# A state-space scan and an ELU layer on one core: seven Strassen products in float32, or three passes over 12-bit words

## The chip, the cores and the metric

The kernel runs on one core of a Trainium2 chip. The metric is the time on the device in microseconds (us). A core has TensorE (PE, with PEld for its weight loads), VectorE (DVE), ScalarE (ACT), GpSimd (POOL) and SyncE (SP), which issues most DMAs. Each engine takes its instructions strictly in the order in which the kernel wrote them, and waits on semaphores for what another engine has to finish first.

## What is computed

Two things in a row, cut to what matters:

```python
# 1. scan: x (4, 8, 768, 32), a (4, 8, 768), B and C (4, 8, 768, 16)
M = (C @ B.T) * L                      # L[i, j] = exp(cum_i - cum_j), j <= i
y = M @ x + (C @ state) * exp(cum)     # state is carried from chunk to chunk
# 2. two layers over the 3072 tokens, 256 features each (8 heads x 32)
h = y @ w_in                           # w_in (256, 2048)
g = np.where(h > 0, h, np.exp(np.minimum(h, 0)) - 1)
out = g @ w_out                        # w_out (2048, 256)
```

The weights are given in 64 bits; the kernel turns them into float32 first.

## The kernel before

The 3072 tokens are 12 blocks of 256 tokens (`BLK`), numbered 0 to 11. For each block the scan makes y as `yT` (features on the partitions), the first layer makes `g_of`, the second layer the output rows. All is one program in an order written out by hand (`manual_schedule`): the scan of later blocks, the first layer of this pair and the second layer of the pair before are woven into each other, piece by piece.

- **Start.** Blocks 0 to 3 use plain float32 products in the first layer (`l1`, L658). Meanwhile the 64-bit weights are loaded in 16 pieces and converted (`w_take`, `w_give`; the magnitude `mag`, the sign `sgn`, the low part, joined by POOL at L239).
- **Blocks 2 and 3** weave `l1` with the second layer of 0 and 1 (`l2`, L779). With block 3, `more_sums` makes sums of the weights for what follows: DVE those of w_out (L706), POOL those of w_in.
- **Pairs (4,5), (6,7), (8,9), (10,11).** This is the loop `for n in range(4, NP, 2)`. Its 16 half steps k do the first layer of the pair by Strassen's scheme: `front`, `mid` and `back` do seven products of 128 x 128 by 128 x 256 for each of eight feature pairs i (all through `part_product`, L730), with sums joined on DVE (L747, L755, L763) and one copy on ACT (L740). `sum_y` makes the sums of y on POOL. `begin_elu` and `elu` make g: Relu (L671) and Exp (L678) on ACT, the join on DVE (L680). `sum_t1` subtracts quarters of g on POOL (L807).
- **Second layer in the same loop**, for the pair before (`second`, L853): seven products in two halves of four chunks each, also by Strassen's scheme. One `next` of this generator, called by `l2s`, does one chunk: two products of 128 x 128 by 128 x 128. Between them POOL subtracts (L795) and adds (L831), DVE adds what stands in PSUM (L831), and ACT copies two of the results (L860, L872).
- **Scan of the next pair in the same loop**: decays by ACT (`decay`, L512, 32 pieces of 64 columns twice, masked by POOL at L517), at k = 10 `scores` (L532), `sums` of the states (L562), `weigh` (DVE, L541) and `states`, and at k = 13 `across` (L607) and `inside` (L626), whose results ACT copies to `yT` (L643).

PSUM has eight banks of 128 x 512 float32. Seven of them are one ring that all temporary results share in the order in which they are asked for; the eighth belongs to the second layer:

```python
p_a = ctx.enter_context(tc.tile_pool(name="ps_a", bufs=7, space=PSUM))
p_o = ctx.enter_context(tc.tile_pool(name="ps_o", bufs=1, space=PSUM))
def psum(shape, name):
    return p_a.tile(shape, F32, tag="a", name=name)
```

A tile asked for waits until the one that had its bank seven requests earlier has been read for the last time. `scores` asks for four banks, `sums` for two, `across` for four, a Strassen step for two.

Of the kernel before, what the change touches and what calls it, by code (L numbers as in the profile page):

```python
# [12 lines left out]
BF16 = mybir.dt.bfloat16  # L13
ALU = mybir.AluOpType
ACT = mybir.ActivationFunctionType

P = 128
Q = 64
BLK = 2 * P
CW = 256  # L20

# [7 lines left out]
def kernel(  # L29
# [56 lines left out]
    la0 = const.tile([P, 2, P], F32, name="la0")  # L86
# [50 lines left out]
    def load_x(n, piece=None):  # L137
        b, g = place(n)
        st[n]["x"] = raw.tile([P, 2, NH * D], F32, tag="xr", name="xr", bufs=4)
        for u in range(2):  # L140
            sl = slice((2 * g + u) * P, (2 * g + u + 1) * P)
            nc.sync.dma_start(  # L142
                out=st[n]["x"][:, u].rearrange("p (h d) -> p h d", d=D),
                in_=x[b, :, sl, :].rearrange("h s d -> s h d"))
            if piece is not None and u == 0:
                w_load(piece)


    w_in = const.tile([P, KC, DF], F32, name="w_in")
# [3 lines left out]
    for i in range(DF // CW):  # L153
        pieces.append((
            w_in[:, :, i * CW:(i + 1) * CW],
# [6 lines left out]
    W_AHEAD = 8  # L162
# [18 lines left out]
    def w_abs(i, cols=slice(None)):  # L181
        if i in (1, 2) or cols.start:
            w_abs_of[i, cols.start] = psum([P, 2, CW], "ps_mag").bitcast(U32)
        if i not in w_mag:
            w_mag[i] = (ffn.tile([P, 2, CW], U32, tag="tmp", name="mag", bufs=1) if i == 2 else
                        conv.tile([P, 2, CW], U32, tag="mag", name="mag"))
# [19 lines left out]
    def w_sign(i, cols=slice(None), eng=nc.vector):  # L206
        if i not in w_sgn:
            w_sgn[i] = conv.tile([P, 2, CW], U32, tag="sgn", name="sgn")
# [54 lines left out]
    keep = const.tile([P, 2, P], F32, name="keep")  # L263
# [30 lines left out]
    heads = [const.tile([P, NH, N], F32, name=f"heads{n}") for n in range(2)]  # L294
# [31 lines left out]
    F0 = const.tile([P, 2, P], F32, name="F0")  # L326
# [68 lines left out]
    def scaled(n, eng):  # L395

        s = st[n]
        s["sc"] = sc = att.tile([P, 2, NH, N], F32, tag="sc", name="sc", bufs=2)
# [15 lines left out]
    def turn(n):  # L414
# [8 lines left out]
        s["bt"] = att.tile([P, 2, 2, P], F32, tag="bct", name="bct", bufs=2)[:, 0]  # L423
# [7 lines left out]
    def turn_exp(n, eng=nc.vector):  # L431

        s = st[n]
        s["cts"] = att.tile([P, 2, P], F32, tag="cts", name="cts", bufs=2)
# [180 lines left out]
    def inside(y, *ns):  # L615


        for t in range(2):
# [16 lines left out]
            for v in range(2):  # L635
                k = shift(n, v)
                for at in (0, k) if k else (0,):
                    count, src = P - k, (at + k) % P
                    to, src = out[at:at + count, :, :, Q * v:Q * v + Q], y[t][v][src:src + count]
                    if t and n == 1:  # L640
                        nc.vector.tensor_copy(to, src)
                    else:
                        nc.scalar.copy(out=to, in_=src)  # L643
# [6 lines left out]
    def l1(n, i, parts=1):  # L650

        ps = psum([P, 2, BLK], "ps_h")
        for j in range(2):
            m = 2 * i + j
            for part in range(parts):
                toks = slice(part * BLK // parts, (part + 1) * BLK // parts)
                for k in range(KC):
                    nc.tensor.matmul(  # L658
                        out=ps[:, j, toks], lhsT=w_in[:, k, m * P:(m + 1) * P],
# [52 lines left out]
    w_parts = w_in.rearrange("p k (i r c) -> p k r i c", r=2, c=P)  # L712
    a_in = a11, a12, a21, a22 = [w_parts[:, k, r] for r in range(2) for k in range(2)]
    w_parts = w_out.rearrange("p (i k) (r c) -> p k r i c", k=2, c=P)
    a_out = [w_parts[:, k, r] for r in range(2) for k in range(2)]
    s_in, s_out = [], []

    y_sums = {}

    def sum_y(n):  # L720
        t = y_sums[n] = conv.tile([P, 4, BLK], F32, tag="w64", name="y_sum", bufs=W_AHEAD)
        b11, b12, b21, b22 = (
            yT[n // 2][:, k, at].rearrange("p u i -> p (u i)") for k in range(2) for at in range(2))
        for r, (in0, in1) in enumerate(((b12, b11), (b22, t[:, 0]), (b22, b12), (b21, t[:, 1]))):
            nc.gpsimd.tensor_tensor(out=t[:, r], in0=in0, in1=in1, op=ALU.subtract)

    open_ = {}

    def part_product(out, lhsT, rhs, first=False):
        nc.tensor.matmul(  # L730
            out=out, lhsT=lhsT, rhs=rhs, start=first, stop=True, skip_group_check=True)
# [3 lines left out]
    def front(n, i):  # L735
        c1, c2 = psum([P, 2, BLK], "ps_h"), psum([P, 2, BLK], "ps_h")
        t = y_sums[n]
        part_product(c1[:, 0], a11[:, i], yT[n // 2][:, 0, 0].rearrange("p u i -> p (u i)"), True)
        u = conv.tile([P, 3, BLK], F32, tag="mag", name="u_sum")
        nc.scalar.copy(out=u[:, 0], in_=c1[:, 0])  # L740
        part_product(c2[:, 0], s_in[0][:, i], t[:, 1], True)
        part_product(c2[:, 1], a21[:, i], t[:, 0])
        open_[n, i] = c1, c2, u

    def front_sums(n, i):
        c1, c2, u = open_[n, i]
        nc.vector.tensor_tensor(  # L747
            out=u[:, 1:3], in0=c2, in1=u[:, 0].unsqueeze(1).to_broadcast([P, 2, BLK]), op=ALU.add)

    def mid(n, i):  # L750
        c1, c2, u = open_[n, i]
        b21 = yT[n // 2][:, 1, 0].rearrange("p u i -> p (u i)")
        part_product(c1[:, 0], a12[:, i], b21)
        part_product(c2[:, 0], s_in[1][:, i], y_sums[n][:, 2])
        nc.vector.tensor_tensor(out=c1[:, 1], in0=c2[:, 0], in1=u[:, 2], op=ALU.add)  # L755
        lag.append((n, i, c1))

    def back(n, i):
        c1, c2, u = open_.pop((n, i))
        b22 = yT[n // 2][:, 1, 1].rearrange("p u i -> p (u i)")  # L760
        part_product(c2[:, 0], a22[:, i], y_sums[n][:, 3])
        part_product(c2[:, 1], s_in[2][:, i], b22)
        nc.vector.tensor_tensor(out=c2, in0=c2, in1=u[:, 0:2], op=ALU.add)  # L763
        lag.append((n + 1, i, c2))
# [7 lines left out]
    def l2(n, j, half=None):  # L772
# [10 lines left out]
        if j == MC // 2 - 1 and half != 0:  # L783
            ob = ffn.tile([P, 2, DM], F32, tag="ob", name="ob", bufs=1)
# [12 lines left out]
    def quarters(n, i):  # L797


        A, B = g_of[n, i], g_of[n + 1, i]  # L800
        if n < 4:
            return A[:, 0], A[:, 1], B[:, 0], B[:, 1]
        return A[:, 0], B[:, 0], B[:, 1], A[:, 1]
# [273 lines left out]
    ends = {(3, 13): (4, 5), (4, 13): (6, 7), (6, 13): (8, 9), (8, 13): (10, 11)}  # L1077

    def end_of_two(n, step):
# [227 lines left out]
```

## Time and profile before

| | |
|---|---|
| median of three runs | 354.9 us (354.79 to 355.4) |
| span of the profiled execution | 353.3 us |
| what lies around the span, against the median | 1.6 us |
| granted TensorE clock | 1.000 |
| first product of the loop over pairs | 115.1 us from the span's start |
| last products, L839, the end of the second layer | 349.8 us from the span's start |

A profile's group row names the line, the engine, the operation, what is written from what, the shape and the count; then the busy time of the group and the mean ns of one instruction; then the idle time of that engine just before them, with what ended it. A timeline row has the start, the length and the instructions merged into it. A matmul's row shows its end with the pipeline's drain, so the rate is read from start to start. A float32 product appears as two matmul records.

### The profile page before, as it was taken

The numbers are of one execution on the slowest core, as the hardware profiler recorded it, in microseconds if no ns is written. First come the engines' busy times: TensorE is split into PE (matmuls) and PEld (weight loads), VectorE is DVE, ScalarE is ACT, GpSimd is POOL, SyncE is SP. The second block draws the span as 40 slices with busy tenths as digits, with TensorE's granted clock in tenths as the row PEclk, the third lists the DMA queues.
The fourth block names the chain that finished last, engine by engine and source line by source line (L and its number), as shares of the span: only waits on it lengthen the run. The fifth ranks groups of instructions, "written<-read, shape, count | busy, mean of one in ns | idle before, by whom it ended". The sixth has DMA issues, their size and how long they took to land.

```text
span 353.3 us, 9964 instructions
## 1 busy us (share of the span) xinstructions
PE 346.3 (98%) x3958; PEld 312.6 (88%) x3958; DVE 239.4 (68%) x497; ACT 204.3 (58%) x497; POOL 231.5 (66%) x366
## 2 busy tenths in 40 slices
PE   8799999999999999999999999999999999999996
PEld 5579888888888999999999999999999999999996
DVE  4898979863999768684677684677684565656212
ACT  4789989787435577535677535586635444535100
POOL 5554554563676997887377788468687545465883
PEclk9999999999999999999999999999999999999999
DMA  8988987550450500145500145600000100000001
GB/s 147 235 213 216 284 206 183 118 98 30 71 142 2 121 1 2 19 99 125 123 0 2 13 82 137 134 3 0 2 2 4 60 3 0 2 0 30 32 2 59
DMA packets 72726, 26.49 MB, mean 75 GB/s; under 512 B 57768, under 2 KB 67560, under 8 KB 72680
## 3 DMA queue, kind: packets, MB, share of 16 engines
q1 hardware_dynamic: 70360, 25.60, 31.5%
q8 instruction: 31, 0.51, 0.6%
q10 hardware_dynamic: 2320, 0.26, 0.5%
q14 instruction: 15, 0.12, 0.1%
HBM read 22.51 MB, written 3.34 MB: 73 GB/s over the span
## 4 chain that ended last, share of the span: by engine, by line
PE 92%; DVE 2%; DMA 2%; SPq 2%; issue 0%; POOL 0%; ACT 0%; DVEq 0%; POOLq 0%; ACTq 0%
PE ps_o L853 35%; PE ps_h L730 28%; PE ps_h L658 15%; PE ps_o L779 8%; PE ps_y L626 2%; DMA w<-in_moe_w_in_dram 2%; PE ps_g L532 2%; PE ps_y L607 1%; PE ps_st L562 1%; SPq L169 1%; PE ps_o L839 1%; POOL w_in L239 0%; DVE sgn L214 0%; DVE ps_mag L222 0%; SPq L142 0%
## 5 line engine op out<-in xcount | busy, mean ns | idle before, releaser
L671 ACT ACTIVATE e<-ps_h 128x512 f32<-128x512 f32 x96 | 57.1, 595 | 91.0 <-DVE ps_h L755 49.3
L853 PEld LDWEIGHTS ps_o<-w_out,g 128*128 128x128 f32 x640 | 79.9, 192 | 2.9
L853 PE MATMUL ps_o<-w_out,g 128*128 128x128 f32 x640 | 81.0, 275 | 0.0
L680 DVE SCALAR_TENSOR_TENSOR g<-e,ps_h 128x512 f32<-128x512 f32 x96 | 65.1, 680 | 14.3 <-ACT e L678 13.7
L658 PE MATMUL ps_h<-yT,w_in 128*128 128x256 f32 (+1 forms) x272 | 60.4, 370 | 2.9 <-POOL w_in L239 2.9
L678 ACT ACTIVATE e<-e 128x512 f32<-128x512 f32 x96 | 60.9, 635 | 2.0
L807 POOL TENSOR_TENSOR g<-g 128x256 f32<-128x256 f32 x33 | 24.0, 728 | 54.8 <-DVE g L680 54.7
L658 PEld LDWEIGHTS ps_h<-yT,w_in 128*128 128x128 f32 x272 | 48.4, 190 | 10.4 <-POOL w_in L239 4.0
L512 ACT ACTIVATE L<-L,ncum 128x64 f32<-128x64 f32 x160 | 41.1, 338 | 0.2
L853 PE MATMUL ps_o<-w_sum,g 128*128 128x128 f32 x304 | 39.9, 275 | 0.0
L853 PEld LDWEIGHTS ps_o<-w_sum,g 128*128 128x128 f32 x304 | 38.5, 192 | 1.1
L763 DVE TENSOR_TENSOR ps_h<-ps_h,u_sum 128x512 f32<-128x512 f32 x32 | 22.4, 698 | 24.0 <-PE ps_h L730 23.8
L730 PE MATMUL ps_h<-yT,w_in 128*128 128x256 f32 x128 | 38.5, 383 | 0.0
L730 PE MATMUL ps_h<-y_sum,w_in 128*128 128x256 f32 x128 | 38.2, 380 | 0.0
L730 PE MATMUL ps_h<-y_sum,w_sum 128*128 128x256 f32 x128 | 38.1, 379 | 0.0
L517 POOL TENSOR_SCALAR_AFFINE_SELECT L<-L 64x512 f32<-64x512 f32 x40 | 28.0, 700 | 11.9 <-ACT L L512 10.6
L747 DVE TENSOR_TENSOR u_sum<-ps_h,u_sum 128x512 f32<-128x512 f32 x32 | 22.1, 689 | 14.7 <-ACT u_sum L740 11.0
L755 DVE TENSOR_TENSOR ps_h<-ps_h,u_sum 128x256 f32<-128x256 f32 x32 | 13.8, 433 | 25.9 <-PE ps_h L730 25.8
L779 PE MATMUL ps_o<-w_out,g 128*128 128x256 f32 x128 | 30.7, 382 | 0.0
L795 POOL TENSOR_TENSOR t<-g 128x256 f32<-128x256 f32 x40 | 28.9, 754 | 0.2
L795 POOL TENSOR_TENSOR g<-g,t 128x256 f32<-128x256 f32 x40 | 28.8, 753 | 0.3
L795 POOL TENSOR_TENSOR g<-t,g 128x256 f32<-128x256 f32 x40 | 27.9, 733 | 1.1 <-PE ps_o L853 1.1
(120 smaller groups left out, 534.8 us busy)
## 6 DMA issues: line engine op xcount, KB each, us to landing
L<-flat SPq DMA_DIRECT2D x20, 256.0 KB
w<-in_moe_w_out_dram SPq DMA_DIRECT2D x8, 512.0 KB
w<-in_moe_w_in_dram SPq DMA_DIRECT2D x7, 512.0 KB
xr<-in_x_dram SPq DMA_DIRECT2D x24, 128.0 KB
out_dram<-c_sum SPq DMA_DIRECT2D x9, 256.0 KB
bc<-in_B_dram SPq DMA_DIRECT2D x24, 64.0 KB
bc<-in_C_dram SPq DMA_DIRECT2D x22, 64.0 KB
ec<-flat_exp SPq DMA_DIRECT2D x10, 128.0 KB
```

Source lines behind the costliest of these rows:

```text
L512: nc.scalar.activation(L[:, h, u], L[:, h, u], ACT.Exp, bias=ncum[:, u, row:row + 1])
L517: nc.gpsimd.affine_select(out=part, in_=part, pattern=[[0, 4], [0, 2], [1, Q]], compare_op=ALU.is_ge, fill=0.0, base=0, channel_multiplier=-1)
L658: nc.tensor.matmul(out=ps[:, j, toks], lhsT=w_in[:, k, m * P:(m + 1) * P], rhs=yT[n // 2][:, k, n % 2].rearrange("p u i -> p (u i)")[:, toks],
L671: nc.scalar.activation(begun[0], lag[0][2], ACT.Relu, scale=-1.0)
L678: nc.scalar.activation(e, e, ACT.Exp, scale=-1.0)
L680: nc.vector.scalar_tensor_tensor(out=g_of[n, i], in0=e, scalar=1.0, in1=ps, op0=ALU.subtract, op1=ALU.max)
L730: nc.tensor.matmul(out=out, lhsT=lhsT, rhs=rhs, start=first, stop=True, skip_group_check=True)
L763: nc.vector.tensor_tensor(out=c2, in0=c2, in1=u[:, 0:2], op=ALU.add)
L779: nc.tensor.matmul(out=o_of[n][:, ts], lhsT=g_of[n, j][:, m % 2, ts * P:(ts + 1) * P], rhs=w_out[:, m], start=(m == 0 and ts == 0), stop=( ...
L795: nc.gpsimd.tensor_tensor(out=out, in0=in0, in1=in1, op=ALU.subtract)
L807: eng.tensor_tensor(out=b12, in0=b12, in1=b11, op=ALU.subtract)
L853: nc.tensor.matmul(out=ps[:, ts], lhsT=b[:, ts * P:(ts + 1) * P], rhs=a[:, i], start=(i == chunk[0] and ts == 0), stop=(i == chunk[-1]), s ...
```

## The change

The first layer of blocks 4 to 11 is done with three products of words in place of Strassen's seven products. A weight w is written as w1 + w0 with w1 rounded to 12 bits (`words_of_w`), y likewise as high and low words (`words_of_y`); y has been multiplied by 2^12 when it was copied out of PSUM. `l1_words` multiplies high by high, low by low, and (high + low) by (high + low), the last into a bank of its own, as Karatsuba's scheme does. All operands have the type float32r and the products have 512 columns, both blocks of the pair at once. The two banks are joined by ACT and DVE, and the ELU follows; the last step of it (`end_words`) is written one tile later.

Other parts that move with it: `w_in` is no longer one tile but eight pieces in a ring of nine that later holds `w0`; the ring `w64` has 11 buffers instead of 8 and later holds the weights' words; `mag` and `sgn` of the conversion take their buffers from the rings of g; `y1` and `y0` have one buffer, `both` shares the two buffers of `yT`; `first` and `bct` gather small tiles; x has three buffers in place of four; `load_bc` for later blocks is called two steps later; `end_of_two`, which ends the scan of a pair and now splits its y, stands at k = 14.

The diff, cut to its core:

```diff
-        st[n]["x"] = raw.tile([P, 2, NH * D], F32, tag="xr", name="xr", bufs=4)
+        st[n]["x"] = raw.tile([P, 2, NH * D], F32, tag="xr", name="xr", bufs=3)
...
-    W_AHEAD = 8
+    W_AHEAD = 11
...
+                    elif n < 4:
+                        nc.scalar.copy(out=to, in_=src)
                     else:
-                        nc.scalar.copy(out=to, in_=src)
+                        nc.scalar.activation(to, src, ACT.Copy, scale=WORD)
...
-    def sum_y(n):
...
-    def front(n, i):
...
-    def front_sums(n, i):
...
-    def mid(n, i):
...
-    def back(n, i):
...
+    def words_of_w(i):
+        w = pieces[i][0]
+        both = conv.tile(
+            [P, 2, KC, CW], F32R, tag="w64", name="w_words", bufs=W_AHEAD)
+        nc.scalar.activation(both[:, 0], w, ACT.Copy, scale=NEAR)
+        nc.vector.scalar_tensor_tensor(
+            out=both[:, 1], in0=both[:, 0].bitcast(F32), scalar=1.0 / WORD - 1.0, in1=w,
+            op0=ALU.mult, op1=ALU.add)
+        w0 = conv.tile([P, KC, CW], F32R, tag="w_in", name="w0", bufs=DF // CW + 1)
+        nc.gpsimd.tensor_tensor(out=w0, in0=w, in1=both[:, 0].bitcast(F32), op=ALU.subtract)
+        k_words[i] = both, w0
...
+    def words_of_y(n):
+        y = yT[n // 2].rearrange("p k b u i -> p k (b u i)")
+        y1 = conv.tile([P, KC, 2 * BLK], F32R, tag="y1", name="y1", bufs=1)
+        y0 = conv.tile([P, KC, 2 * BLK], F32R, tag="y0", name="y0", bufs=1)
+        both = ffn.tile([P, KC, 2 * BLK], F32R, tag="yT", name="y_both")
+        for k in range(KC):
+            nc.scalar.activation(y1[:, k], y[:, k], ACT.Copy, scale=NEAR / WORD)
+            nc.vector.scalar_tensor_tensor(
+                out=y0[:, k], in0=y1[:, k].bitcast(F32), scalar=WORD, in1=y[:, k],
+                op0=ALU.mult, op1=ALU.subtract)
+            nc.vector.scalar_tensor_tensor(
+                out=both[:, k], in0=y1[:, k].bitcast(F32), scalar=1.0 - WORD,
+                in1=y[:, k], op0=ALU.mult, op1=ALU.add)
+        y_words[n] = y1, y0, both
+
+    def l1_words(n, m):
...
+        high, both = psum([P, 2 * BLK], "ps_h"), psum([P, 2 * BLK], "ps_w")
+        for k in range(KC):
+            nc.tensor.matmul(
+                out=both, lhsT=both_w[:, k], rhs=both_y[:, k], start=k == 0, stop=k == KC - 1)
+        for k in range(KC):
+            nc.tensor.matmul(
+                out=high, lhsT=w1[:, k], rhs=y1[:, k], start=k == 0, stop=False)
+            nc.tensor.matmul(
+                out=high, lhsT=w0[:, k], rhs=y0[:, k], start=False, stop=k == KC - 1)
+        e = ffn.tile([P, 2 * BLK], F32, tag="e", name="e", bufs=2)
+        nc.scalar.copy(out=e, in_=both)
+        nc.vector.scalar_tensor_tensor(
+            out=high, in0=high, scalar=1.0 - 1.0 / WORD, in1=e, op0=ALU.mult, op1=ALU.add)
+        nc.scalar.activation(e, high, ACT.Relu, scale=-1.0)
+        nc.scalar.activation(e, e, ACT.Exp, scale=-1.0)
+        late.append((n, m, high, e))
...
+    def end_words():
+        n, m, h, e = late.pop(0)
+        g_of[n, m] = ffn.tile([P, 2, BLK], F32, tag=f"g{m % 2}", name="g", bufs=12)
+        nc.vector.scalar_tensor_tensor(
+            out=g_of[n, m].rearrange("p b i -> p (b i)"), in0=e, scalar=1.0, in1=h,
+            op0=ALU.subtract, op1=ALU.max)
+        if m % 2 == 0:
+            sub(g_of[n, m][:, 1], g_of[n, m][:, 1], g_of[n, m][:, 0])
...
-        if n % 2 == 1 and i in (1, 3) and n + 3 + i // 2 < NP:
-            load_bc(n + 3 + i // 2)
+        if n % 2 == 1 and i in (3, 5) and n + 3 + i // 4 < NP:
+            load_bc(n + 3 + i // 4)
...
         sum_weights(nc.vector, a_out, s_out, i)
-        sum_weights(nc.gpsimd, a_in, s_in, i)
+        words_of_w(i)
...
         for k in range(16):
...
+            if m and k == 10:
+                l2s(4)
+                end_words()
+                scores(m, m + 1)
+                sums(m, m + 1)
+                for q in range(3):
+                    weigh_two(m, q)
+                states(m)
                 l2s(2)
+                l1_words(n, k)
+                weigh_two(m, 3)
             else:
+                l1_words(n, k)
+                if len(late) > 1:
+                    end_words()
+                turn_step(n, k // 2 * 2 + 1, k % 2)
+                if m and k == 11:
+                    states(m + 1)
+                l2s((4, 3)[k % 2] if k < 8 or not m else (2, 3, 0, 1, 2, 2, 2, 2)[k - 8])
...
+            if m and k == 14:
+                l2s(1)
+                end_words()
+                end_of_two(m, m + 1)
+        end_words()
         for _ in steps:
             pass
```

## The prediction

> **What bounds the kernel now.** I read the page's busy times and chain first, then the chain in order of time, then the busy times by stretch, then the timeline at the places that the change touches.
>
> ```profile
> PE 346.3 (98%) x3958; PEld 312.6 (88%) x3958; DVE 239.4 (68%) x497; ACT 204.3 (58%) x497; POOL 231.5 (66%) x366
> PE ps_o L853 35%; PE ps_h L730 28%; PE ps_h L658 15%; PE ps_o L779 8%; PE ps_y L626 2%; DMA w<-in_moe_w_in_dram 2%; PE ps_g L532 2%; PE ps_y L607 1%; PE ps_st L562 1%; SPq L169 1%; PE ps_o L839 1%; POOL w_in L239 0%; DVE sgn L214 0%; DVE ps_mag L222 0%; SPq L142 0%
> ```
>
> TensorE is busy 98% and its products are the chain. L730, Strassen's seven products, is 28% of the span: what the change replaces. The chain in order of time gives prices and a period:
>
> ```profile
> 140.96 1.78 PE ps_o L853 x16
> 154.10 2.16 PE ps_h L730 x10
> 194.66 1.78 PE ps_o L853 x16
> ```
>
> A float32 product leaves two records. So a product of 256 columns costs 2.16/5 = 0.432 us, a second-layer product of 128 columns 1.78/8 = 0.2225 us, one step of the second layer (two products) 0.445 us. The same step comes back after 194.66 - 140.96 = 53.7 us: the time of a pair of blocks. There are four such pairs, (4,5) to (10,11); the first three also prepare the next pair's scan. Busy times over the seven steps before the first pair, and over one period:
>
> ```profile
> 87.50:115.10 27.60, 27.60 (x413) 23.85 (x412) 25.90 (x61) 12.30 (x28) 18.84 (x37) 1.00 0.32 71
> 141.00:194.70 53.70, 53.70 (x642) 49.99 (x641) 37.64 (x78) 32.14 (x83) 38.91 (x60) 1.00 0.29 60
> ```
>
> (columns: length, then busy us of PE, PEld, DVE, ACT, POOL). In the period PE has no gap, and ScalarE (ACT) works 32.1 of 53.7 us. But before the first pair VectorE (DVE) has only 1.7 us of 27.6 left.
>
> **TensorE's share of the change.** Removed: 7 products x 8 steps x 4 pairs = 224 of 256 columns, x 0.432 = 96.8 us. Added: 6 x 16 x 4 = 384 of 512 columns in float32r, a type that before.py never uses. Its bounds lie in two rows, one-pass bf16 and a float32 product, both of 256 columns:
>
> ```profile
> 14.47 0.60 PE L472 MATMUL ps_x<-low,ident 128*128 128x256 bf16 x4
> ```
> ```profile
> 181.33 0.59 PE L730 MATMUL ps_h<-y_sum,w_sum 128*128 128x256 f32 x2
> ```
>
> Four bf16 records take 0.60 us of which the last one's own 0.27 overlaps nothing: 0.33/3 = 0.11 us each, a quarter of 0.432. So float32 costs four passes and one pass streams 256 columns in 0.108. Bounds for 512 columns: 0.216 (one pass) to 0.865 (four). [...] On PE alone the change is worth 96.8 - 82.9 = 13.9 us. Everything now depends on whether the others keep up.
>
> **What one output tile costs ScalarE.** Before, a step's three TensorE results were joined on DVE, and ACT did one 256-column copy and two Relu/Exp pairs. Now each tile m of 128 features x 512 tokens sends a chain back and forth through queues that run in order: ACT copies `both` (ps_w), DVE joins it with `high`, ACT does Relu, then Exp. The prices are in these rows of one step and of single forms:
>
> ```profile
> 180.65 0.70 DVE L763 TENSOR_TENSOR ps_h<-ps_h,u_sum 128x512 f32<-128x512 f32 x1 [0.32 <-PE ps_h L730]
> 181.39 0.60 ACT L671 ACTIVATE e<-ps_h 128x512 f32<-128x512 f32 x1 [0.64 <-DVE ps_h L763]
> 181.88 0.37 ACT L740 COPY u_sum<-ps_h 128x256 f32<-128x256 f32 x1
> 182.13 0.64 ACT L678 ACTIVATE e<-e 128x512 f32<-128x512 f32 x1
> 182.67 2.01 ACT L512 ACTIVATE L<-L,ncum 128x64 f32<-128x64 f32 x8
> ```
> ```profile
> L785 ACT COPY ob<-ps_o 128x512 f32<-128x512 f32 x2 | 1.1, 575 | 0.4 <-PE ps_o L779 0.4
> L763 DVE TENSOR_TENSOR ps_h<-ps_h,u_sum 128x512 f32<-128x512 f32 x32 | 22.4, 698 | 24.0 <-PE ps_h L730 23.8
> L807 POOL TENSOR_TENSOR g<-g 128x256 f32<-128x256 f32 x33 | 24.0, 728 | 54.8 <-DVE g L680 54.7
> L452 DVE TENSOR_TENSOR ctm<-bct,hmask 128x512 f32<-128x512 f32 x9 | 8.3, 925 | 0.0
> ```
>
> The handoff DVE to ACT is 0.04 (180.65 + 0.70 to 181.39); an Exp lets the next instruction start after 0.54 (182.13 to 182.67); a decay exponential (L512) costs (2.01 - 0.34)/7 = 0.24. Nothing stands between copy and Relu on ACT, so it idles while DVE joins: 0.575 + 0.03 + 0.70 + 0.03 + 0.60 + 0.03 + 0.54 = 2.50 us per tile, against 1.30 us of TensorE products and its second-layer steps.
>
> **Where that lands on TensorE.** Count from a pair's first product. By the order written in the loop, tiles 0 to 9 go with 33 second-layer steps: PE 10 x 1.30 + 33 x 0.445 = 27.7 us. In that stretch ACT also has the next pair's 32 decays, 7.7 us, and two copies of ps_o (0.27 each). ACT therefore begins tile 9's copy at 0.6 (first `both` done) + 9 x 2.50 + 7.7 + 0.5 = 31.3 us. Until here seven PSUM banks, two per tile, soak up the lag. They end at tile 10: the scores take four banks and the state sums two, so the second bank of the sums is the one that holds tile 9's `high`. Four more steps (1.8) and the scores (1.1) bring PE there at 30.6. The bank comes free only when DVE has written tile 9's g, and DVE's queue has in front of that an add into c_sum which waits for POOL; POOL's queue has six adds of 0.73 before it is done, the first of them on tile 8's g. In before this stands as follows, with no wait in it:
>
> ```profile
> 146.16 0.75 POOL L831 TENSOR_TENSOR c_sum<-c_sum,p_sum 128x256 f32<-128x256 f32 x1
> 146.94 0.42 DVE L831 TENSOR_TENSOR c_sum<-ps_o,c_sum 128x256 f32<-128x256 f32 x1
> 147.08 1.21 PE L532 MATMUL ps_g<-ctm,bct 32*64 32x128 f32 x64
> 147.43 0.69 DVE L680 SCALAR_TENSOR_TENSOR g<-e,ps_h 128x512 f32<-128x512 f32 x1
> ```
>
> After: join of tile 9 at 31.9, g of tile 8 from 32.5 to 33.2, POOL's six adds to 37.6, DVE's add 0.34, g 0.68: 38.6. PE waits 38.6 - 30.6 = 8.0 us, three times. Behind tile 10 the lag is gone, since PE then has more than ACT (scan products, 19 steps). For the later waits of the same kind (the four ps_y banks behind tiles 13 and 14) I take 1.3 us, between 0 and one tile cycle of 2.5.
>
> **Where pairs begin.** y is split into words by two ACT and four DVE passes of 512 columns. y1 and y0 have one buffer, so the split waits for the last tile's products; 18 second-layer products (18 x 0.2225 = 4.0 us) cover 0.6 + 4 x 0.69 = 3.4 us, but DVE's adds for ps_o stand behind the passes: 0.8 us per begin, between 0 and the passes' 2.8. For the first pair no steps stand between, `both` takes the yT buffer that l1(3,7) still reads, and the weights' words put seven DVE passes (0.69, L452's shortest) = 4.8 us into the stretch that has 1.7 left. DVE is 3.1 late when l1(3,7) ends, and two to four of its y passes lie behind that: 3 to 5.9 us if both add up; I take 4, since some of the passes fall into the stretch. [...] The 925 mean against 0.69 is what I keep for the upper end.
>
> **Hidden:** the subtractions of g on POOL are as many as before (eight per pair, L807), sum_y's 16 leave POOL, and the w0 passes (1.3 by L239's form) replace four of 0.52 each; POOL has 53.7 - 38.9 = 14.8 us of room per period, and without it each subtraction (0.73) would be late by itself. B's and C's loads are issued two steps later on SP's queue, and x keeps three tiles in place of four: the next pair's turns that read them come over ten us later, TensorE waits for no DMA in this stretch, and a late landing would cost its own few us per pair. The conversion of the weights only moves to other buffers; I cost it nothing, bounded by the 2.9 us that PE waits there now (L658 behind w_in).
>
> **The sum:** -13.9 + 4 + 3 x (8.0 + 1.3 + 0.8) = +20.4 us (three pairs prepare a next one, and three begin behind another). The profiled execution spans 353.3, which is 1.6 below the median of 354.9; around it nothing changes. 354.9 + 20.4 = 375.3.
>
> **Rivals.** *ACT does not hold PE (faster).* If the lag stays inside the seven banks, only the first begin is paid: 354.9 - 13.9 + 4 = 345. That needs a tile cycle under (27.7 - 8.2)/10 = 1.95 us in place of 2.50. For it: ACT's 32.1 of 53.7 us; against: those are busy times, and the chain's idle 0.76 per tile is not in them. *The bank comes back without the detour over POOL.* Then g of tile 9 ends at 31.3 + 0.6 + 0.73 + 0.63 + 0.66 + 0.68 = 34.6, the wait is 4.0, and the time 375.3 - 12 = 363. Against: the order on DVE's queue. *float32r is no single pass.* At half a float32 product, 0.432, PE does 165.9 us, +69.1; ACT then keeps up and waits of some 3 us at the scores stay: 354.9 + 69 + 4 + 9 = 437; at 0.865 about 600.
>
> **Numbers.** Forecast 0.70; without POOL 0.12; longer waits through contended passes (16 x 0.24 = 4 us, and up to 15 more if all of ACT's and DVE's prices are some 5% higher, since each 0.1 us on the tile cycle counts ten times in each of three pairs) 0.05; ACT in time 0.07; more than one pass 0.05; no change at all 0.01. The range runs from below the case without POOL, 360, to 396. Under 0.2% this kernel's measurement tells nothing from no change. Faster 0.07, same 0.01, slower 0.92.
>
> **What would show it.** Right: period 60 us or more in place of 53.7; PE's largest waits on the state sums (ps_st) and scores behind DVE, ACT's busy share up, DVE waiting for POOL's c_sum. A product of float32r near 0.22 us. Wrong: PE still without gaps in 141 to 194, or records of 0.43 us.

## The result and the profile after

The changed kernel takes **394.5 us** (median of four runs, 393.76 to 396.08) beside 354.9 for the kernel before: a ratio of 1.112, 95% interval 1.110 to 1.115. It is slower by 39.6 us. The forecast was slower by 20.4 (375.3, range 360 to 396): the sign and the place are right, the size is half. The profiled execution took 396.08 us, with a span of 394.4 and a granted clock of 0.952.

The page after, its busy times and two of its rows by slices:

```profile
PE 357.2 (91%) x3894; PEld 310.0 (79%) x3894; DVE 240.1 (61%) x489; ACT 238.8 (61%) x545; POOL 216.9 (55%) x326
PE   8899999999967997599899588998949899999996
PEclk9999999999996999599999869999968999999999
```

TensorE is still the busiest, but now with holes: one at slices 12 and 13 (the first pair's begin), then three at like distances (slices 17, 23 and 30). The granted clock falls at or just behind each of them; in before it was 1.000 throughout. The holes come back with the pairs. In the chain in order of time the same step, the second layer's first products behind the state sums, is found at

```profile
164.16 2.00 PE ps_o L883 x8
229.02 2.00 PE ps_o L883 x8
294.47 2.01 PE ps_o L883 x8
```

that is 64.9 and 65.4 us apart, where before had 53.7 and the prediction's sum gave 60.3. By the starts of the timeline rows this step is at 164.09, 228.95 and 294.40 us (span 394.4), and in before at 149.00, 202.70 and 256.35 (span 353.3). So the 41.1 us between the two spans fall into four parts: 15.1 before the first of these marks, 11.2 and 11.8 in the two periods, 3.0 behind the last.

What TensorE waits for, and two waits of DVE and ACT, in the list of waits (total us, times, longest):

```profile
ACT e L780 <- DVE ps_h L778: 66.5, 64, 2.2
DVE c_sum L861 <- POOL c_sum L861: 19.2, 6, 4.3
PE ps_st L567 <- DVE g L789: 11.4, 3, 4.0
PE ps_w L769 <- DVE y_both L756: 6.2, 2, 4.8
PE ps_g L537 <- DVE g L789: 2.7, 3, 0.9
```

The first row is ScalarE standing idle in each of the 64 tiles while DVE joins, about one us a tile. Where nothing else disturbs a tile, ACT's rows show the cycle that the prediction priced (copy, a wait of 0.77 for the join, Relu, Exp), from 137.50 to 140.02 here, 2.52 us:

```profile
137.50 0.59 ACT L777 COPY e<-ps_w 128x512 f32<-128x512 f32 x1
138.85 0.60 ACT L780 ACTIVATE e<-ps_h 128x512 f32<-128x512 f32 x1 [0.77 <-DVE ps_h L778]
139.48 0.63 ACT L781 ACTIVATE e<-e 128x512 f32<-128x512 f32 x1
140.02 2.00 ACT L517 ACTIVATE L<-L,ncum 128x64 f32<-128x64 f32 x8
```

The second and third row of the list of waits are the detour that the prediction drew: TensorE's state sums wait for tile 9's g on DVE, DVE's queue stands behind its add into `c_sum`, and this add waits for POOL. The timeline of the first begin and of k = 10 in the first pair shows each step, and further down what a product costs when nothing waits:

```profile
116.50 4.56 POOL L824 TENSOR_TENSOR t<-g 128x256 f32<-128x256 f32 x4
117.02 1.20 DVE L753 SCALAR_TENSOR_TENSOR y<-y,yT 128x512 fp32r<-128x512 f32 x1
119.50 0.76 PE L769 MATMUL ps_w<-y_both,w_words 128*128 128x512 f32 x1 [4.80 <-DVE y_both L756]
121.67 0.79 PE L769 MATMUL ps_w<-y_both,w_words 128*128 128x512 f32 x1 [1.41 <-DVE y_both L756]
122.71 0.69 DVE L736 SCALAR_TENSOR_TENSOR w_words<-w_words,w_in 128x512 fp32r<-128x512 f32 x1
...
154.72 0.43 PE L537 MATMUL ps_g<-ctm,bct 32*64 32x128 f32 x4
156.35 0.43 PE L537 MATMUL ps_g<-ctm,bct 32*64 32x128 f32 x2 [1.20 <-ACT e L777]
157.67 1.16 PE L537 MATMUL ps_g<-ctm,bct 32*64 32x128 f32 x58 [0.89 <-DVE g L789]
157.79 0.73 POOL L824 TENSOR_TENSOR g<-g 128x256 f32<-128x256 f32 x1 [0.50 <-DVE g L789]
158.49 2.76 POOL L824 TENSOR_TENSOR g<-t,g 128x256 f32<-128x256 f32 x4
161.21 0.72 POOL L861 TENSOR_TENSOR c_sum<-c_sum,p_sum 128x256 f32<-128x256 f32 x1
161.96 0.42 DVE L861 TENSOR_TENSOR c_sum<-ps_o,c_sum 128x256 f32<-128x256 f32 x1 [4.34 <-POOL c_sum L861]
162.31 0.68 DVE L789 SCALAR_TENSOR_TENSOR g<-e,ps_h 128x512 f32<-128x512 f32 x1
163.04 1.12 PE L567 MATMUL ps_st<-xr,b_tok 64*32 64x64 f32 x56 [3.96 <-DVE g L789]
164.09 2.08 PE L883 MATMUL ps_o<-w_out,g 128*128 128x128 f32 x8
167.24 0.63 PE L774 MATMUL ps_h<-y,w 128*128 128x512 f32 x1
167.66 0.63 PE L772 MATMUL ps_h<-y,w_words 128*128 128x512 f32 x1
...
332.10 1.05 PE L883 MATMUL ps_o<-w_sum,t 128*128 128x128 f32 x8
332.99 1.06 PE L883 MATMUL ps_o<-w_sum,g 128*128 128x128 f32 x8
333.80 0.70 PE L769 MATMUL ps_w<-y_both,w_words 128*128 128x512 f32 x2
334.34 0.40 PE L772 MATMUL ps_h<-y,w_words 128*128 128x512 f32 x1
335.27 1.05 PE L883 MATMUL ps_o<-w_sum,g 128*128 128x128 f32 x8
```

Read it so. The scores wait for banks of the ELU, first for ACT's copy of tile 9's `both` (1.20), then for tile 8's g (0.89). The moment g of tile 8 is there, POOL starts its six operations (157.79 to 161.93), DVE adds (161.96), makes g of tile 9 (162.31), and TensorE goes on at 163.04: 3.96 us lost. Then comes what the prediction did not have. The eight products of 164.09 take 2.08 where they take 1.05 later on, and two float32r products start 167.66 - 167.24 = 0.42 us apart. The granted clock in the windows around fell with it (columns: length, busy us of PE, PEld, DVE, ACT, POOL; then granted clock, DMA share, GB/s):

```profile
141.00:206.00 65.00, 57.01 (x628) 49.63 (x627) 36.67 (x73) 39.69 (x94) 36.24 (x57) 0.92 0.24 50
115.00:118.00 3.00, 0.00 (x0) 0.00 (x0) 3.00 (x5) 1.02 (x2) 2.75 (x3) 1.00 0.49 158
118.00:124.00 6.00, 3.10 (x7) 2.14 (x8) 5.90 (x11) 0.59 (x1) 3.06 (x3) 0.51 0.59 98
157.00:160.00 3.00, 1.40 (x66) 1.07 (x66) 0.62 (x2) 1.49 (x3) 2.50 (x5) 0.85 0.02 5
160.00:169.00 9.00, 5.96 (x72) 5.12 (x73) 4.15 (x13) 0.59 (x1) 5.84 (x11) 0.50 0.21 31
```

At k = 10 the granted clock is halved about when the long wait begins (0.85 over 157 to 160 is full speed up to about 159.1), and stays so for about six us after TensorE has resumed (163.04 to 169). At the first begin the half clock comes later in the stop: TensorE has nothing to do from 114.7 on, the clock is full to 118 (1.00 over 115 to 118), halved right behind (0.52 over 118 to 121), and back at about 125 (0.84 over 124 to 127), 3.3 us after the work goes on at 121.67. At k = 10 it falls as the wait of 3.96 begins, behind four us (155 to 159, clock 1.00) in which TensorE was busy for 1.90.

The lines from 332.10 price a tile at full clock: from 332.10 to 335.27 stand four second-layer steps (4 x 0.445 = 1.78 us) and one tile, 3.17 - 1.78 = 1.39 us.

### The profile page after: what moved, and what is told of

It is laid out like the page before. It is cut to its first block, busy times and chain, and to the rows that moved or that the text cites. A ratio compares the mean times of both kernels' runs of the same rounds, so it can differ in the third digit from the quotient of the medians.

```text
span 394.4 us, 9900 instructions
## 1 busy us (share of the span) xinstructions
PE 357.2 (91%) x3894; PEld 310.0 (79%) x3894; DVE 240.1 (61%) x489; ACT 238.8 (61%) x545; POOL 216.9 (55%) x326
## 4 chain that ended last, share of the span: by engine, by line
PE 58%; ACT 14%; DVE 14%; issue 6%; POOL 3%; SPq 2%; DMA 1%; DVEq 0%; POOLq 0%; ACTq 0%
PE ps_o L883 21%; PE ps_h L665 13%; PE ps_o L808 7%; DVE ps_h L778 4%; PE ps_w L769 4%; PE ps_h L774 4%; PE ps_h L772 4%; ACT L L517 4%; ACT e L780 4%; ACT e L777 3%; DVE g L789 3%; POOL g L824 2%; PE ps_y L631 1%; DMA w<-in_moe_w_in_dram 1%; PE ps_st L567 1%
## 5 line engine op out<-in xcount | busy, mean ns | idle before, releaser
L778 DVE SCALAR_TENSOR_TENSOR ps_h<-ps_h,e 128x512 f32<-128x512 f32 x64 | 44.7, 699 | 81.1 <-ACT e L777 43.7
L883 PEld LDWEIGHTS ps_o<-w_out,g 128*128 128x128 f32 x640 | 80.7, 198 | 6.8 <-DVE c_sum L861 3.7
L883 PE MATMUL ps_o<-w_out,g 128*128 128x128 f32 x640 | 83.2, 283 | 2.4 <-DVE c_sum L861 2.4
L780 ACT ACTIVATE e<-ps_h 128x512 f32<-128x512 f32 x64 | 38.3, 598 | 66.5 <-DVE ps_h L778 66.5
L777 ACT COPY e<-ps_w 128x512 f32<-128x512 f32 x64 | 36.7, 573 | 32.7 <-PE ps_w L769 32.3
L769 PE MATMUL ps_w<-y_both,w_words 128*128 128x512 f32 x128 | 48.3, 459 | 6.2 <-DVE y_both L756 6.2
L772 PE MATMUL ps_h<-y,w_words 128*128 128x512 f32 x128 | 52.5, 410 | 0.3 <-ACT e L777 0.3
L774 PE MATMUL ps_h<-y,w 128*128 128x512 f32 x128 | 52.3, 408 | 0.0
L789 DVE SCALAR_TENSOR_TENSOR g<-e,ps_h 128x512 f32<-128x512 f32 x64 | 43.4, 679 | 4.6 <-ACT e L781 4.6
L883 PE MATMUL ps_o<-w_sum,g 128*128 128x128 f32 x304 | 39.5, 276 | 2.8 <-DVE p_sum L861 2.1
L883 PEld LDWEIGHTS ps_o<-w_sum,g 128*128 128x128 f32 x304 | 37.6, 192 | 5.1 <-PE ps_o L883 2.6
L781 ACT ACTIVATE e<-e 128x512 f32<-128x512 f32 x64 | 40.4, 631 | 2.0
L772 PEld LDWEIGHTS ps_h<-y,w_words 128*128 128x128 f32 x128 | 25.5, 199 | 8.0 <-ACT e L777 1.6
L824 POOL TENSOR_TENSOR t<-g 128x256 f32<-128x256 f32 x40 | 30.4, 791 | 0.0
L774 PEld LDWEIGHTS ps_h<-y,w 128*128 128x128 f32 x128 | 25.2, 197 | 5.8
```

The source lines that it names most:

```text
L769: nc.tensor.matmul(out=both, lhsT=both_w[:, k], rhs=both_y[:, k], start=k == 0, stop=k == KC - 1)
L772: nc.tensor.matmul(out=high, lhsT=w1[:, k], rhs=y1[:, k], start=k == 0, stop=False)
L774: nc.tensor.matmul(out=high, lhsT=w0[:, k], rhs=y0[:, k], start=False, stop=k == KC - 1)
L777: nc.scalar.copy(out=e, in_=both)
L778: nc.vector.scalar_tensor_tensor(out=high, in0=high, scalar=1.0 - 1.0 / WORD, in1=e, op0=ALU.mult, op1=ALU.add)
L780: nc.scalar.activation(e, high, ACT.Relu, scale=-1.0)
```

## The experiments

Each run has the kernel before on the same chip beside it (355.2, 354.9, 355.0 and 355.0 us in the four groups). Two theories stood against each other: the 19 us by which the forecast was too low come from the halved clock behind the waits, or from ELU results that simply come later than priced.

**Fill the waits with work (e1).** Dummy products keep TensorE busy before the first tile of the first pair and before each state sum.

```diff
+        if len(ns) == 2 and ns[0] > 4:      # sums
+            for _ in range(8):
+                nc.tensor.matmul(out=ps[0]..., lhsT=minus, rhs=w_out[:, 15], ...)
...
+        for _ in range(11 if (n, m) == (4, 0) else 0):      # l1_words
+            nc.tensor.matmul(out=both[:, 0:BLK], lhsT=minus, rhs=w_out[:, 15], ...)
```

> The same kernel, but TensorE gets work in its four longest waits: 11 products of 256 columns (4.8 us) before the first tile of pair (4,5), and 8 (3.5 us) before the state sums of each next pair; they write into banks that the real products then overwrite. Theory 1, the part of the loss that the prediction missed is TensorE's clock: it falls to 0.50 behind each of these waits (119.5 to 125 and 159.7 to 169.5 in the profile after) and the products that follow run at half speed. TensorE then has about 4.5 us of half-speed work at the first begin and 6 us in each of three pairs, so half of it, 2 + 3 x 3 = 11 us, comes back: 383 us and a mean clock above 0.98. Theory 2, the whole loss is waits on other engines: the waits last as long as before, the clock changes nothing on the path, 394 us.

Measured: 390.6 us, ratio 1.101 (1.097 to 1.104), mean clock 0.987. So most of the clock came back and only 4 us with it. In the windows the clock still falls behind the scores' waits, ahead of the dummies:

```profile
157.00:160.00 3.00, 2.49 (x59) 2.09 (x60) 0.45 (x1) 1.39 (x3) 2.50 (x5) 0.52 0.04 11
```

At that half clock the dummies themselves last too long: in the second pair the eight take 5.41 us (3.5 by the 0.432 of the prediction), and the state sums start at 227.21, although tile 9's g was written by 226.1.

```profile
221.88 5.41 PE L564 MATMUL ps_st<-w_out,minus 128*128 128x256 f32 x16
227.21 0.87 PE L572 MATMUL ps_st<-xr,b_tok 64*32 64x64 f32 x64
```

In the first pair they cost 0.7 us in the same way, in the third nothing, so some 2 us of what the clock gave back went into the dummies. For the rest my reading, not shown by a run of its own, is that TensorE that runs faster afterwards meets the same lagging ELU sooner. Neither expectation is met in full.

**Take the detour away (e2).** At k = 10 `end_words` (tile 9's g) is written ahead of the second-layer steps whose add waits for POOL.

```diff
-                l2s(4)
                 end_words()
+                l2s(4)
```

> At half step 10 the last step of the ELU of tile 9 is written before the four steps of the second layer, not behind them. So on VectorE tile 9's g no longer stands behind the add into c_sum that waits for GpSimd. Theory 1, as the prediction's rival has it: the bank of the state sums comes 4 us earlier in each of three pairs, and with that the clock does not fall: 12 us for the waits, up to 9 for the clock, 374 to 382 us. Theory 2: the whole of VectorE's queue is held by that add, the weighing too, so the banks of the scores come back just as late and tile 10 waits in place of the state sums: 392 to 394 us, with the wait on ps_w in place of ps_st.

Measured: 387.0 us, 1.090 (1.087 to 1.093): 7.6 us less, between the two theories. The list of waits shows where the rest went:

```profile
PE ps_w L769 <- DVE M L546: 4.4, 3, 2.2
PE ps_g L537 <- DVE g L789: 2.7, 3, 0.9
```

The wait for the state sums is gone (11.4 us), but the blocked add now stands in front of `weigh`, whose M frees the scores' banks: a new wait of 4.4 us. And what the scores wait for is untouched.

**Take ScalarE's idle time away (e3).** ACT copies tile m, then does Relu and Exp of tile m - 1, so nothing waits for DVE's join.

```diff
         nc.scalar.copy(out=e, in_=both)
...
-        nc.scalar.activation(e, high, ACT.Relu, scale=-1.0)
-        nc.scalar.activation(e, e, ACT.Exp, scale=-1.0)
+        relu_exp()                    # of the tile before
         late.append((n, m, high, e))
+        joined.append((high, e))
```

> ScalarE's order in a tile is changed: it copies tile m, then does Relu and Exp of tile m - 1, whose join VectorE has finished meanwhile. So the 0.77 us in which ScalarE waits for the join in every tile are filled, and a tile takes it 0.48 + 0.50 + 0.54 = 1.5 us in place of 2.5. Theory 1, the chain back and forth makes ScalarE late: 10 tiles save 10 us of its time in a pair, its lag before the scores is gone, the waits of the scores (about 2 us) and on ps_o vanish, and only the wait for GpSimd's queue before the state sums (about 4 us, with the clock's fall) stays: 394.5 - 3 x (2 + 2 + 1.5) = 378 us. Theory 2, ScalarE has room and GpSimd or VectorE alone sets the waits: within 2 us of 394.

Measured: 382.0 us, 1.075 (1.073 to 1.077): 12.6 us less. The scores' waits vanish from the list; the detour stays, a little longer since TensorE now arrives earlier:

```profile
PE ps_st L567 <- DVE g L799: 13.0, 3, 4.4
```

**Take ScalarE's other work away (e4).** The decays of blocks 6 to 11 are left out.

```diff
-        for u in range(2):
+        for u in range(2 if n < 6 else 0):
```

> The decay exponentials of ScalarE (L517) are left out for blocks 6 to 11; everything else is as in the changed kernel. Theory 1, chain and decays together make the lag: without the 7.7 us of decays ScalarE keeps pace with ten tiles (25 us against 27.7 us of TensorE), the scores wait for nothing, GpSimd's masking no longer waits for ScalarE, and the state sums wait less than 4 us: 372 to 380 us. Theory 2, the lag comes from GpSimd's subtractions and adds alone: the state sums wait as long as before, at most 3 us in all are gained, 391 to 394 us.

Measured: 377.4 us, 1.063 (1.060 to 1.066), 17 us less, as theory 1 had it: the 7.7 us of decays that ScalarE has in each of three pairs do lie on the path. The state sums still wait 2.54 us each, and behind that shorter wait the products ran at half rate too (eight of L883 in 2.08):

```profile
216.62 1.02 PE L567 MATMUL ps_st<-xr,b_tok 64*32 64x64 f32 x56 [2.54 <-DVE g L789]
217.57 2.08 PE L883 MATMUL ps_o<-w_out,g 128*128 128x128 f32 x8
```

**Reorder k = 10, alone and with e3 (e6, e5).** The order becomes `end_words`, two steps, scores, sums, `weigh`, `states`, and only then the four steps with the add that waits for POOL.

```diff
-                l2s(4)
                 end_words()
+                l2s(2)
...
-                l2s(2)
+                l2s(4)
```

> Only the second of the two: at half step 10 the end of tile 9's ELU goes first, then two steps of the second layer, the scores, sums, weighing and states, then four steps; ScalarE's order in a tile is as in the changed kernel. Theory 1, ScalarE's lag and GpSimd's queue add up: the wait for ps_st behind VectorE's add (4 us, with the clock's fall behind it) goes and the lag stays, 3.5 to 4 us of waits at the scores: 394.5 - 3 x (4 + 1.3) = 378 us. Theory 2, the lag is all there is and GpSimd's detour lies beside it: 390 us or more.

> Both orders are changed: ScalarE copies tile m before Relu and Exp of tile m - 1, and at half step 10 tile 9's ELU ends first, two steps of the second layer go before the scores and four behind the states, so that VectorE's add into c_sum, which waits for GpSimd, stands behind the weighing. Theory 1, the two orders together are the whole of the waits in the three pairs: each period is TensorE's own work, 53.7 less what the word products save (with 1.40 us a tile in place of the 1.30 of the prediction: 1.8 us) plus about 1 us at each begin, so 53 us; only the first begin's 6 us and the clock's fall behind it stay: 354.9 - 7 + 3 + 8 = 359 us. Theory 2, queues give it back elsewhere (ps_y, ps_o): periods of 57 us or more, 370 us.

Measured: e6 382.6 us, 1.076 (1.072 to 1.080), 11.9 less; e5 364.1 us, 1.028 (1.025 to 1.031), **30.4 less**. One alone gives 11.9, the other 12.6, both together 30.4 rather than 24.5. My reading is that while either stays, TensorE still stops near k = 10 in each pair: in e3 4.41 us at the state sums, in e6 up to 2.1 us at the scores. In e5 the list shows no wait for an ELU result any more, and its clock is 0.990. What remains is mostly the first begin, 4.91 + 1.40 us there.

**Ease the first begin as well (e7).** To e5 are added: seven steps of the second layer ahead of the first tile, the one subtraction of `sum_t1` in each step before it moved from DVE to POOL, the passes for `both` ahead of those for y0, and the y0 products last in a tile.

```diff
+                if n == 4 and k == 0:
+                    l2s(7)
...
-        sum_t1(2, i, nc.vector)
+        sum_t1(2, i)
```

> As e5_pipe_late, with three changes at the first begin: seven steps of the second layer go before the first tile of pair (4,5) and none behind its first two tiles; one subtraction per step before it (sum_t1) moves from VectorE to GpSimd; of the y words, both passes for high + low come before those for low, and the two products with y0 come last in a tile. Theory 1, the first begin's 6 us of wait and the half clock behind it (about 8 us in all) are hidden by the steps in front: 351 to 354 us, at or just below the kernel before. Theory 2, VectorE is late all the same and the steps only move the wait: within 2 us of e5_pipe_late.

Measured: 364.0 us, 1.025 (1.024 to 1.027), clock 1.000: no better than e5. TensorE's waits at the first begin shrink to 0.54 + 0.65 + 0.17 + 0.65, and then it waits 3.6 us in the first tiles: 1.04 + 0.87 for their ELU results and 1.07 + 0.63 for partial sums that ACT and DVE have to read first. With the clock at 1.000, whatever is left of the loss is not the clock.

**Is it float32r's price? (e8)** The e7 kernel, with the upper halves of the words read as bf16.

```diff
+        w1, both_w, w0, y1, y0, both_y = (
+            [t[:, k].bitcast(BF16).rearrange("p (c h) -> p c h", h=2)[:, :, 1] for k in range(KC)]
+            for t in (w1, both_w, w0, y1, y0, both_y))
```

> As e7_all, but the six products of a tile read the upper halves of the same words as bf16: every product loses the lower bits of its operands. Their count, columns and order are the same. In the changed kernel a tile takes TensorE about 1.40 us where six passes of 512 columns at 0.213 are 1.28, and its weight loads last 0.20 us each where those of bf16 lasted 0.10 to 0.15. Theory 1, the excess is float32r's weight load, which does not hide behind a short product: with bf16 a tile takes 1.30 us, 64 x 0.10 = 6 us less than e7_all. Theory 2, the excess is the accumulation or the issue of any product: the same time within 1 us.

Measured: 362.9 us, 1.0225 (1.0206 to 1.0245), 1.0 less than e7, with intervals that overlap. In its timeline a tile between steps takes 1.35 us (bf16) beside 1.40 in e7 (float32r): a product in this company costs about 0.225 to 0.235 us. The 0.213 of the expectation is half of the 0.427 that lie between such products at half clock (in after four of them start at 122.26, 122.69, 123.11 and 123.54). The prediction's 0.216 came from a row of four bf16 products alike, with nothing of another shape between them.

**Add TensorE work (e9, e10).** One spare pass per tile, 128 products at 0.23 = 29.4 us, in the changed kernel and in e7.

```diff
+        for k in range(KC):
+            nc.tensor.matmul(
+                out=both, lhsT=w0[:, k], rhs=y0[:, k], start=k == 0, stop=k == KC - 1)
```

> The changed kernel with one spare pass per tile: low word by low word a second time, into the bank of `both`, which the true pass then overwrites; the values stay. That is 128 more float32r products of 512 columns at 0.23 us, 29.4 us of TensorE. Theory 1 (the changed kernel waits in the pairs for ELU results that lag behind TensorE, so a longer tile is partly filled into these waits: about 25 us of them in three pairs, and the clock would no longer fall): the time rises by far less than 29.4, to 398 to 410 us. Theory 2 (TensorE's own work and the waits add up, because the waits hang on the order of the queues at k = 10 and not on the lag): 394.5 + 29 = 424 us.

> The kernel with the mended order (ELU a tile later, k = 10 reordered, first begin eased; it ran at 364.0) with the same spare pass. Theory 1 (with the waits gone TensorE alone sets the time): all 29.4 us are paid, 364.0 + 29.4 = 393 us, to within 2 us. Theory 2 (another engine still sets part of the time): 375 to 388 us.

Measured: e9 410.3 us, 1.156 (1.153 to 1.159), 15.8 more, just above the range of theory 1: nearly half of the added work (by the price of 0.23) went into waits. Two rows of the list show which part did so and which did not:

```profile
PE ps_st L567 <- DVE g L792: 11.9, 3, 4.0
PE ps_g L537 <- DVE g L792: 0.9, 3, 0.3
```

The scores' wait, which is lag, shrinks from 2.7 to 0.9; the state sums' wait does not shrink at all. In these two runs it is not lag but order: TensorE waits at the scores for tile 8's g, however shortly, POOL's six operations start at that moment, and 3.95 us follow. e10 took 386.4 us, 1.088 (1.084 to 1.093), 22.4 more than e7 and not 29.4: a quarter of the spare pass was free. So even there TensorE alone does not set the time: theory 2 held, theory 1 did not.

**Take TensorE work away (e11).** The e7 kernel with two products of each tile left out.

```diff
-                out=high, lhsT=w1[:, k], rhs=y1[:, k], start=k == 0, stop=False)
-        for k in range(KC):
-            nc.tensor.matmul(
-                out=high, lhsT=w0[:, k], rhs=y0[:, k], start=False, stop=k == KC - 1)
+                out=high, lhsT=w1[:, k], rhs=y1[:, k], start=k == 0, stop=k == KC - 1)
```

> The kernel with the mended order with the pass low word by low word left out (the product is then incomplete: values lose their lowest part). 128 products less. Theory 1 (TensorE alone sets the time, also with tiles a third shorter): 364.0 - 29.4 = 334.6 us, 20 us faster than before. Theory 2 (ScalarE's tile cycle becomes the bound once the products are a third shorter, as in the prediction's step on ScalarE: copy, Relu and Exp are 1.8 us a tile against 1.0 of products, plus 7.7 us of decays at each tenth tile): a gain of only 10 to 20 us, 344 to 354 us, with new waits of TensorE on DVE's g or ScalarE.

Measured: 359.7 us, 1.012 (1.009 to 1.014): only 4.3 us for a third of the products, a smaller gain than either theory had. The clock, 0.981 in the profiled execution, is little of it: the one execution at 1.000 took 358.2. ScalarE's timeline shows the second bound, and the list of its waits the ring behind it:

```profile
135.79 0.56 ACT L776 COPY e<-ps_w 128x512 f32<-128x512 f32 x1
139.97 2.00 ACT L517 ACTIVATE L<-L,ncum 128x64 f32<-128x64 f32 x8
141.88 0.56 ACT L776 COPY e<-ps_w 128x512 f32<-128x512 f32 x1
```
```profile
ACT e L776 <- DVE g L798: 20.0, 27, 0.8
```

Two tiles with their decays take 141.88 - 135.79 = 6.09 us, and in e7, where a tile has six products instead of four, 6.08 (134.08 to 140.16). TensorE needs about 2 x 1.40 + 6.6 steps x 0.445 = 5.7 us for the same in e7. So in this stretch the two bounds lie close together, ScalarE's being the longer.

**Three buffers of e (e12).** The e7 kernel, in which ACT's copy no longer waits for DVE's g of two tiles ago.

```diff
-        e = ffn.tile([P, 2 * BLK], F32, tag="e", name="e", bufs=2)
+        e = ffn.tile([P, 2 * BLK], F32, tag="e", name="e", bufs=3)
-        ... name="g", bufs=12)
+        ... name="g", bufs=11)
```

> The kernel with the mended order (364.0) with three buffers of e (the tile that ScalarE's copy writes) in place of two; the 2 KB come from the two rings of g, 11 buffers each in place of 12. ScalarE waited 13.9 us there for DVE's g to read an e. Theory 1 (the ring of e holds ScalarE, and through it TensorE, in the first tiles of a pair): the waits of the copy for g shrink to under 4 us, and 2 to 5 us of the 9 us by which this version is slower than before go: 359 to 362 us. Theory 2 (TensorE's own work is the whole of it: its products in this version are as long as Strassen's within 2 us, and the waits that remain are of other kinds): 363 to 365 us, no change.

Measured: 360.6 us, 1.017 (1.014 to 1.019), as theory 1 had it: 3.4 less than e7, and the copy's waits for g (13.9 us in e7) are gone from ScalarE's list; two tiles with decays take it 5.2 to 5.5 us. e11 with three buffers was not run. The state sums of two following pairs stand at

```profile
207.00 0.94 PE L567 MATMUL ps_st<-xr,b_tok 64*32 64x64 f32 x64
```

and at 260.34 us: a period of 53.3 us, beside 53.8 in before (201.91 to 255.69). In this period the kernel with three passes is 0.4 us faster. The period ahead of it takes 54.4 (from 152.57) beside 53.7 (from 148.21), with a wait of 2.36 us in it:

```profile
177.58 2.02 PE L895 MATMUL ps_o<-w_out,g 128*128 128x128 f32 x16 [2.36 <-DVE c_sum L873]
```

So over the two periods nothing is gained. And the first state sums come at 152.57 instead of 148.21, 4.4 us late: in the begin of the first pair stand waits of 0.55 + 0.64 + 0.18 + 0.65 for the words, then 0.34 + 0.63 + 1.08 in the first tiles, 4.1 us together. It is the fastest version with all products, and still 5.6 us slower than the kernel before.

## Why the prediction was right in sign and too small

**Products.** Mis-sized. The 82.9 us of the sum are 384 products at the lower of the two bounds, 0.216, by my estimate that one pass is enough; no run shows that price in a tile. The runs show 1.39/6 = 0.232 a product in after, near that bound and far from 0.432 and 0.865, so the rival of more than one pass is out. A tile of six takes 1.39 us, not 1.30, so TensorE's gain is 96.8 - 64 x 1.39 = 7.8 us, not 13.9: 6 us of the miss. In e8's timeline half of the excess stays with bf16.

**ScalarE's cycle of 2.50 us.** Right: an undisturbed tile has it, with 0.77 us idle for the join (over all 64 tiles the mean is 66.5/64 = 1.04), and e3 and e4 show that both the idle time and the decays count. Taking away one or the other gave 12.6 and 17 us.

**The waits in a pair.** Right in kind and place, a little too large: the forecast had 10.1 us a pair. TensorE idles 8.0 and 8.1 us in the two periods: 3.96 and 3.53 for the state sums, 1.46 at the scores (2.09 in the first pair), the rest in smaller waits, for c_sum and p_sum above all. Over the three pairs it is 25 us where 30.3 were forecast. The prediction put the whole wait at the bank of tile 9; a part of it lies at the scores, for tile 8. That detail matters: in e9 the lag is smaller and the state sums wait 3.95 us all the same; with tile 9's g behind the add, only the run without the decays (e4) has less, 2.54.

**The rival without the detour.** Its price of 12 us was too big for the swap alone: e2 gave 7.6, since the blocked add then holds `weigh`. The waiting add does not vanish by standing elsewhere in its queue (4.4 us of new waits in e2); only behind everything that TensorE needs (e5, e6) did it stop to count.

**First begin.** 4.80 + 1.41 = 6.2 us, not 4: each of the four passes over y took 1.20 or 1.21 us beside POOL's subtractions, while the same kind of pass at 122.71 took 0.69. The forecast had 0.69 for each, and 0.925 only in the upper end of its range. POOL's four subtractions were slower there too: 4.56 us, 1.14 each, where one at 157.79 takes 0.73. That the two engines slow each other is my reading of these rows; no run separates them. 4 x 0.51 = 2.0 us is about the miss.

**The clock.** Not in the sum at all: every wait was priced with TensorE at full speed behind it. Counted from start to start in the trace it is about 2.9 us a pair (eight second-layer products 0.8 more, the first tile behind them 1.3, the state sums and the second tile 0.4 each) and 1.5 at the first begin, 10.2 us together; e1 gave 4 of them back.

**The sum again.** One more term shows in the trace. A product's row ends later than the next can start (the eight at 332.10 have a row of 1.05 us, and the next eight start 0.89 behind them), so a stop costs more than the idle time listed: scores and state sums take from 154.72 to 164.09, 9.37 us, and 1.92 in before (147.08 to 149.00). Of these 7.45 us 6.05 are listed waits and 0.4 the clock; 1.0 is left for the stops themselves, and as much in the other pairs. For one period: -2.0 for the products, +8.0 waits, +2.9 clock, +1.0 stops = 9.9 of the 11.2 measured. Over the whole the terms moved the forecast by +6.1 (products) + 2.2 (first begin) - 5.3 (waits, three pairs) + 10.2 (clock) + 3.0 (stops) = 16.2 of the 20.7 us by which the spans miss the forecast. The other 4.5 us I cannot place one by one.

**The range.** 394.5 us lies 1.5 below its upper end of 396, and that it does is partly luck. That end was set for slower passes and for ACT and DVE prices 5% higher. The slower passes gave about 2 us, those prices held, and most of the miss came from the clock and from the products, which the range had not been made for.

**The rival in which ScalarE keeps up** would probably not have given 345 either. I take e12 as nearly that case, though its order differs: it runs at clock 0.999 and takes 360.6. With the tile at 1.39 and a begin that costs 4.4, there was little to win.

## What to carry to other kernels

When a change makes TensorE's part shorter, price the chain of the other engines per tile with its idle handoffs, not their busy share: here ScalarE's 60% was already a bound. Waits of TensorE can have a second price: in the changed kernel each of its four longest stops, 3.5 to 4.8 us, had the granted clock at half (0.50), for three to six us after the work went on. e4 has this with 2.54 us, but e12 has a wait of 2.36 without it. And in hand-ordered queues look for an instruction that waits for a slow engine in front of one that TensorE needs: moving the ELU by one tile and one such add by some lines gave 30 of the 39.6 us back.

## What was not expected of the hardware

The clock was halved without one long idle stretch. In e4 products ran at half rate after waits of 2.54 us (eight of L883 in 2.08 us, 1.05 at full clock), where the scores' small products (32 x 64 tiles) stood just before. In e1 it fell at about 157.1 (1.00 over 154 to 157, 0.52 over 157 to 160), among such products, after two waits of 1.20 and 0.89; TensorE had been busy for 1.42 of the three us from 154 to 157. Small products are not needed for it: at e1's first begin, with one wait of 1.78 us and products of 128 x 128 alone, the clock was 0.84 from 121 to 124 and 0.60 from 124 to 127. And e12 kept 1.00 (153 to 207) through its wait of 2.36 us. No run here separates what these places have in common from what sets e12 apart. Second, products of 512 columns (L772 and L774, float32r) came 0.225 to 0.235 us apart at full clock and 0.42 to 0.43 at half.
